# Block-sparse attention into a gated MLP: scores of batches 1 to 3 as pairs of 64-row products, their mask as two more

## The chip, the cores and the metric

The kernel runs on one core of one Trainium2 chip. The metric is the device time of one launch in microseconds (us), given as the median of several runs. The core's engines are named as the profile names them: PE is TensorE's matmul stream, PEld its weight loads, DVE VectorE, ACT ScalarE, POOL GpSimd, SP SyncE, which here issues transfers.

## The reference: what is computed

Attention over `q`, `k`, `v` of shape (4 batches, 8 heads, 768 positions, 64), then an MLP with a gate over the positions:

```python
scores = scale * q @ k^T                     # scale = 1/8
scores = where(mask, scores, -1e9)           # mask by blocks of 32 positions
attn   = softmax(scores)
x      = (attn @ v), heads side by side      # (4, 768, 512)
h      = max(x @ w_in, 0);  u, v = halves of h
v_n    = (v - mean(v)) / sqrt(var(v) + 1e-6)
v_s    = w_spatial @ v_n + b_spatial         # over the positions
out    = (u * v_s) @ w_out
```

A query block may look at its own and the neighbouring blocks, at the first and the last block, and at three sampled blocks; the first and last query blocks look at all. The sampled blocks are an input, the same for all batches and heads.

## The kernel before, in words

**The mask inside the score product.** A score needs 64 rows of the array (the head's width). `kq` is the scores' operand, a tile [128 partitions, 8 heads, 768 keys + 768 queries]: rows 0 to 63 hold a head's keys and queries, transposed, and rows 64 to 127 hold mask rows, for the keys a one at their block's row (24 blocks) and for the queries 0 or -300 for that block. One product over all 128 rows so gives score plus mask, and the exponential on ACT (which multiplies by 1/8) turns masked scores into nothing. The mask rows are built once, during batch 0, for each of the eight heads' places (`mask_rows`, line 268, and `rows`, line 236). In `mask_rows` line 269 is called three times; one of its calls uses only the 24 rows from 64 on.

**Slots.** The work is laid out by hand in slots, one loop at the end (line 846). Slots 0 to 35 (S0 = 36) are batch 0, in units cut for an early start. From slot 36 on each slot is one call of `qk_full(j, ci)` (line 422): for head j and one of six chunks of 128 keys, two products give 128 x 768 scores in a PSUM tile `ps` (two buffers), and one exponential writes them to `a_all`. There are 144 such slots, for 24 heads of batches 1 to 3. Seven slots later `av_full(j, qc)` (line 471) takes six products with `a_all` as weights and `vv` as the moving operand, one for each key chunk, to get 128 queries' output (65 columns: 64 and the row sum), and `normalize` (line 438) divides on DVE. Behind that, in the same slot, `run_queue` (line 712) issues MLP products of the batch before, dealt evenly over the slots: on average somewhat over two of up to 512 columns. So a slot's order on PE is: two score products, six value products, some MLP products, and PE takes them in that order.

**How keys and queries get to `kq` from batch 1 on.** The heads go in pairs p (two heads each, 12 slots a pair; `slot_of(p)`, line 808, is the pair's first slot g). SP loads k, q and v, mostly 36 slots ahead; POOL casts them, mostly 24 slots ahead, to bf16 (`nat`, both heads of a pair side by side in 128 columns); `tr_dma(p)` (line 372) has SP issue a transposing transfer, 17 to 19 slots ahead for most pairs (15 for pair 4), into `tt` [128 partitions, 12 chunks, 128], two buffers. In `tt` rows 0 to 63 are the first head of the pair and rows 64 to 127 the second. `split(p, h)` (line 376) copies one head's half on DVE, through `dve_copy` (line 211), into rows 0 to 63 of that head's place in `kq`, three to five slots ahead.

**Queues.** SP's queue holds, in order, the loads, the transposing transfers, the transposes of the attention output (`xtr_dma`, line 507) and the stores.

**Start and end.** At the start PE runs filler products (line 179) until there is work. After the last score slot come the rest of batch 3's MLP products, some 30 us.

Of the kernel before, what the change touches and what calls it, by code (L numbers as in the profile page):

```python
# [10 lines left out]
FP32 = mybir.dt.float32  # L11
BF16 = mybir.dt.bfloat16
I32 = mybir.dt.int32
AF = mybir.ActivationFunctionType
ALU = mybir.AluOpType
# [11 lines left out]
def kernel(  # L27
# [16 lines left out]
    nc = tc.nc  # L44

    B, H, S, D = q.shape
# [3 lines left out]
    NCH = S // 128  # L50
# [6 lines left out]
    NG = H // 2  # L57
# [13 lines left out]
    work = ctx.enter_context(tc.tile_pool(name="work", bufs=1))  # L71
    psum = ctx.enter_context(tc.tile_pool(name="psum", bufs=1, space=bass.MemoryType.PSUM))
# [10 lines left out]
    kq = const.tile([128, H, 2 * S], BF16, name="kq")  # L83
# [3 lines left out]
    MX = slice(D, 128)  # L87
# [95 lines left out]
    def ts(out, in0, s1, o0, s2=None, o1=None):  # L183
        kw = {} if o1 is None else {"op1": o1}
        nc.vector.tensor_scalar(out=out, in0=in0, scalar1=s1, scalar2=s2, op0=o0, **kw)  # L185

    def tt_op(out, in0, in1, op):
        nc.vector.tensor_tensor(out=out, in0=in0, in1=in1, op=op)
# [21 lines left out]
    def dve_copy(o, i):  # L210
        nc.vector.tensor_copy(out=o, in_=i)  # L211
# [158 lines left out]
    tt = {}  # L370

    def tr_dma(p):
        tt[p] = work.tile([128, 2 * NCH, 128], BF16, tag="tt", bufs=2, name="tt")
        nc.sync.dma_start_transpose(out=tt[p], in_=nat.pop(p).rearrange("p c h d -> p (c h d)"))

    def split(p, h):
        src = tt[p].rearrange("x c n -> x (c n)")
        dve_copy(kq[0:D, (2 * p + h) % H, :], src[h * D:(h + 1) * D, :])


    a_ref, av_ref, x_ref, xn_ref, xt_ref = {}, {}, {}, {}, {}

# [4 lines left out]
    def qk_unit(u, e):  # L387
# [31 lines left out]
            ps = ps.rearrange("p (c n) -> p c n", c=len(parts))  # L419
        nc.scalar.activation(out=out, in_=ps, func=AF.Exp, scale=0.125)  # L420

    def qk_full(j, ci):
        if ci == 0:
            a_ref["h", j] = work.tile([128, NCH * S], BF16, tag="a_all", bufs=3,
                                      name="a_all").rearrange("p (c n) -> p c n", c=NCH)
        ps = psum.tile([128, 1024], FP32, tag="sc", bufs=2)
        for n0, n1 in ((0, 512), (512, S)):
            nc.tensor.matmul(out=ps[:, n0:n1],  # L428
                             lhsT=kq[:, j % H, ci * 128:(ci + 1) * 128],
                             rhs=kq[:, j % H, S + n0:S + n1], start=True, stop=True)  # L430
        nc.scalar.activation(out=a_ref["h", j][:, ci, :], in_=ps[:, 0:S], func=AF.Exp, scale=0.125)  # L431

    def av_tile(key, n):
        ps = psum.tile([128, 512], FP32, tag="av", bufs=2, name="ps_av")
        av_ref[key] = ps[:, 0:n * VA].rearrange("p (c d) -> p c d", d=VA)
        x_ref[key] = ps[:, 512 - TW // 2:512].bitcast(BF16)

    def normalize(ps, out, n):
        rc = work.tile([128, NCH, 1], FP32, tag="rc", bufs=2)
        nc.vector.reciprocal(out=rc[:, 0:n], in_=ps[:, :, D:VA])  # L440
        nc.vector.tensor_tensor(out=out, in0=ps[:, :, 0:D],  # L441
                                in1=rc[:, 0:n].to_broadcast([128, n, D]), op=ALU.mult)

    def av_unit(u, e):
        t, p = UNITS[u]
        if e == 0:
            av_tile(u, 2 * TC)
        for i in range(8 * e, 8 * e + 8):
            g, ci = divmod(i, NCH)
            if t == "h":  # L450
                h, qc, to, n = p, g, g, 2 * TC
                pp = 0
            else:
                (h, qc), n, pp = divmod(g, TC), TC, p
                to = qc * 2 + h
            at = (h * NCH + ci) * n * 128 if t != "h" else ci * n * 128
            at += qc * 128
            nc.tensor.matmul(out=av_ref[u][:, to, :], lhsT=a_ref[u][:, at:at + 128],  # L458
                             rhs=vv[pp % NVV][:, h, ci, :],
                             start=(ci == 0), stop=(ci == NCH - 1))  # L460
        if e == 2:
            a_ref.pop(u)
            if t == "h":
                if p == 0:
                    xn_ref[0] = work.tile([128, 2 * TC, 2, D], BF16, tag="xn0", bufs=1, name="xn0")
                normalize(av_ref.pop(u), xn_ref[0][:, :, p, :], 2 * TC)
            else:
                xn_ref[u] = work.tile([128, TC, 2, D], BF16, tag="xn3", bufs=3, name="xn3")
                normalize(av_ref.pop(u), xn_ref[u].rearrange("p c h d -> p (c h) d"), 2 * TC)

    def av_full(j, qc):
        p, h = divmod(j, 2)
        if qc == 0:
            av_tile(j, NCH)
        for ci in range(NCH):
            nc.tensor.matmul(out=av_ref[j][:, qc, :],  # L476
                             lhsT=a_ref["h", j][:, ci, qc * 128:(qc + 1) * 128],
                             rhs=vv[p % NVV][:, h, ci, :],
                             start=(ci == 0), stop=(ci == NCH - 1))
        if qc == NCH - 1:  # L480
            a_ref.pop(("h", j))
            if h == 0:
                xn_ref["p", p] = work.tile([128, NCH, 2, D], BF16, tag="xn", bufs=2, name="xn")
            normalize(av_ref.pop(j), xn_ref["p", p][:, :, h, :], NCH)

    def xt_tile(p):
        if p not in xt_ref:
# [224 lines left out]
    def run_queue():  # L712
        if not queue or pace["slots"] <= 0:
            return
        pace["credit"] += (len(queue) - pace["credit"]) / pace["slots"]
        pace["slots"] -= 1
        n = int(pace["credit"] + 0.5)
        for _ in range(min(n, len(queue))):
            queue.popleft()()
            pace["credit"] -= 1  # L720
# [3 lines left out]
    at, late, pre = {}, {}, {}  # L724

    def when(slot, *fns):
        at.setdefault(slot, []).extend(fns)

    def c(f, *a, **kw):
        return lambda: f(*a, **kw)  # L730
# [77 lines left out]
    def slot_of(p):  # L808
        return S0 + 12 * (p - NG)

    for p in range(NG, NP):
        g = slot_of(p)
        when({4: 14, 5: 20, 6: 28, 11: g - 29, 15: g - 29}.get(p, g - 36), c(load, p, "k"), c(load, p, "q"), c(load, p, "v"))
        when({4: 17, 5: 23, 6: 37, 11: g - 22, 15: g - 22}.get(p, g - 24),
             *[c(cast, p, nm, PL, cs=cs) for nm in "kqv" for cs in (((C01, C23, C45) if p > 5 else (ALLC,)))])
        when({4: 21, 5: 27, 11: g - 18, 15: g - 18, 10: g - 17, 14: g - 17}.get(p, g - 19), c(tr_dma, p))
        if p % NG == 1 and p > 2 * NG:
            late.setdefault(g - 4, []).append(c(split, p, 0))
        else:
            when(g - 5, c(split, p, 0))  # L820
        when(g + 4 if p == NG else g - 3, c(split, p, 1))
        if p == NP - 1:
            when(g + 20, last_x)
        elif p % NG == NG - 1:
            when(g + 19, c(xtr_dma, p))
        else:
            when(g + 20, c(xtr_dma, p))
# [13 lines left out]
    for u in range(len(UNITS)):  # L841
        for e in range(3):
            sl = (5, 6, 6)[e] if u == 0 else 3 * u + e + (4 if u < 3 else 3)
            av_at.setdefault(sl, []).append((u, e))
    NS = S0 + 12 * (NP - NG)
    for s in range(NS + LAG + 2):
        if s < S0:
            qk_unit(*divmod(s, 3))
        elif s < NS:
            j, ci = divmod(s - S0, NCH)  # L850
            qk_full(j + H, ci)
        early = at.get(s, [])
        for f in pre.get(s, []):
            f()
        for u, e in av_at.get(s, []):
            av_unit(u, e)
        if 0 <= s - LAG - S0 and s - LAG < NS:
            j, qc = divmod(s - LAG - S0, NCH)
            av_full(j + H, qc)
        for f in early:  # L860
            f()
        run_queue()
        for f in late.get(s, []):
            f()
        while post:
            post.pop(0)()
# [31 lines left out]
```

## Time and profile before

| what | value |
|---|---|
| median of 3 runs | 210.06 us (209.74 to 210.12) |
| span of the profiled execution, first to last instruction | 208.3 us |
| its own time as a whole | not given; the runs lie 1.4 to 1.8 us above the span |
| instructions | 5489 |
| ACT exponentials of the 144 slots (line 431) | 144 x 812 ns, 113.4 us |
| PE products of the scores (line 428) | 288, 70.3 us with overlaps counted once |
| PE value products (line 476) | 864 of 65 columns |

How to read it: the profile counts an engine's busy time from its instructions' records. Records of PE products overlap, since a product starts before the one before it has ended, and their ends are modelled; the step from one start to the next says what a product costs in a stream. The chain of waits follows the work that ended last back to the start. The granted clock (PEclk) is the share of full speed at which PE was let run. In instruction rows `128*128` is rows x columns of the weights, then the moving operand.

### The profile page before, as it was taken

To read this page: it belongs to the slowest core of one execution; us is meant where nothing else is said; L and a number is where in the kernel's file an instruction comes from. 1 tells how busy PE (TensorE), PEld (TensorE's weight loads), DVE (VectorE), ACT (ScalarE), POOL (GpSimd) and SP (SyncE) were. 2 spreads that over 40 slices of the span, in tenths; PEclk is the share of its full clock that TensorE was granted. 3 is DMA by queue.
4 is the path that set the end of the run, shared out by engine and by line. 5 is a ranking of instruction groups with operands and counts; after the bars stand their busy time and mean duration, and the time that the engine had idled before them with its cause. 6 is when DMAs were issued, how large, how long until landed. Compare 5 with 4: busy or idle time off the path is not lost.

```text
span 208.3 us, 5489 instructions
## 1 busy us (share of the span) xinstructions
PE 201.0 (97%) x2203; PEld 138.0 (66%) x2225; DVE 146.8 (70%) x315; ACT 168.4 (81%) x222; POOL 89.4 (43%) x186
## 2 busy tenths in 40 slices
PE   6899999999999999999999999999999999999993
PEld 6599888777766776667556676667665567445551
DVE  6888776989876766575975585456875666576871
ACT  6899999999999999989899878889899884266021
POOL 6888989767927964006757600006210000013000
PEclk9999999999999999999999999999999999999999
DMA  5999899999999999499987920499402010610016
GB/s 143 338 362 357 275 383 270 206 247 389 253 253 308 259 300 208 139 199 386 292 176 206 139 41 0 164 189 335 75 0 41 0 37 4 250 57 0 0 70 232
DMA packets 53053, 39.48 MB, mean 190 GB/s; under 512 B 33956, under 2 KB 47652, under 8 KB 53028
## 3 DMA queue, kind: packets, MB, share of 16 engines
q1 hardware_dynamic: 52596, 38.74, 70.0%
q10 hardware_dynamic: 432, 0.39, 0.6%
q8 instruction: 17, 0.28, 0.5%
q14 instruction: 8, 0.07, 0.1%
HBM read 24.77 MB, written 6.29 MB: 149 GB/s over the span
## 4 chain that ended last, share of the span: by engine, by line
PE 87%; DVE 4%; ACT 4%; DMA 2%; issue 1%; POOL 0%; ACTq 0%
PE ps L428 21%; PE ps_moe L630 17%; PE ps_moe L561 13%; PE ps_av L476 12%; PE ps L415 7%; PE ps_av L458 4%; PE ps_t L561 4%; PE ps_t L630 4%; PE ps_sc L630 2%; ACT a_all L420 2%; DVE stats L594 2%; DVE vn L185 2%; DMA st_q<-in_q_dram 2%; PE ps_sc L561 1%; PE ps L263 1%
## 5 line engine op out<-in xcount | busy, mean ns | idle before, releaser
L431 ACT ACTIVATE a_all<-ps 128x768 bf16<-128x768 f32 x144 | 113.4, 812 | 13.8 <-PE ps L428 6.2
L428 PE MATMUL ps<-kq 128*128 128x512 bf16 (+1 forms) x288 | 70.3, 326 | 0.3
L476 PEld LDWEIGHTS <-a_all 128*128 128x128 bf16 x864 | 46.6, 98 | 19.0
L476 PE MATMUL ps_av<-vv,a_all 128*128 128x65 bf16 x864 | 51.1, 194 | 0.1
L428 PEld LDWEIGHTS <-kq 128*128 128x128 bf16 x288 | 27.9, 97 | 23.6
L137 POOL CAST nat<-st_k 128x256 bf16<-128x256 f32 (+3 forms) x37 | 17.7, 509 | 38.7 <-DMA st_k<-in_k_dram 38.7
L420 ACT ACTIVATE a_all<-ps 128x1024 bf16<-128x1024 f32 x35 | 33.5, 1027 | 0.3
L630 PE MATMUL ps_moe<-w_spt,vn 128*128 128x512 bf16 (+1 forms) x144 | 33.1, 325 | 0.0
L598 POOL TENSOR_SCALAR std<-mv 128x3 f32<-128x3 f32 (+1 forms) x9 | 3.4, 376 | 48.7 <-DVE mv L595 48.5
L661 DVE TENSOR_TENSOR sb<-ps_moe,b_row 128x512 f32<-128x512 f32 x18 | 12.4, 690 | 14.5 <-PE ps_moe L630 14.2
L630 PE MATMUL ps_moe<-xt,w_in_t 128*128 128x256 bf16 (+1 forms) x108 | 21.7, 299 | 0.2
L415 PE MATMUL ps<-kq 128*128 128x256 bf16 x135 | 20.8, 275 | 0.8 <-DVE kq L211 0.6
L561 PE MATMUL ps_moe<-w_in_t,xt 128*128 128x512 bf16 x65 | 20.2, 378 | 0.2
L137 POOL CAST vv<-st_v 128x256 bf16<-128x256 f32 (+2 forms) x37 | 18.5, 533 | 3.9 <-DMA st_v<-in_v_dram 3.8
L137 POOL CAST nat<-st_q 128x256 bf16<-128x256 f32 (+2 forms) x41 | 19.2, 496 | 1.6 <-DMA st_q<-in_q_dram 1.5
L561 PE MATMUL ps_moe<-w_out_t,un 128*128 128x512 bf16 x64 | 19.4, 378 | 0.2
L441 DVE TENSOR_TENSOR xn<-ps_av,rc 128x384 bf16<-128x384 f32 (+1 forms) x36 | 18.5, 513 | 1.4 <-DVE rc L440 0.2
L664 DVE TENSOR_TENSOR un<-sb,un 128x512 bf16<-128x512 f32 x24 | 17.4, 727 | 1.5
L630 PEld LDWEIGHTS <-vn 128*128 128x128 bf16 x192 | 15.5, 97 | 4.4
L594 DVE BATCH_NORM_STATS2 stats<-vn 128x6 f32<-128x512 bf16 x24 | 16.5, 688 | 1.5 <-ACT vn L589 0.9
L211 DVE COPY osb<-ps_moe 128x512 f32<-128x512 f32 x12 | 8.3, 689 | 11.2 <-PE ps_moe L561 9.3
L211 DVE COPY kq<-tt 64x1536 bf16<-64x1536 bf16 x24 | 15.4, 641 | 0.6 <-DMA tt<-nat 0.2
(94 smaller groups left out, 241.6 us busy)
## 6 DMA issues: line engine op xcount, KB each, us to landing
out_dram<-osb SPq DMA_DIRECT2D x23, 256.0 KB, 2.1
st_k<-in_k_dram SPq DMA_DIRECT2D x15, 384.0 KB, 4.6
st_v<-in_v_dram SPq DMA_DIRECT2D x15, 384.0 KB, 6.2
st_q<-in_q_dram SPq DMA_DIRECT2D x12, 384.0 KB, 4.9
ws_f<-in_moe_w_spatial_dram SPq DMA_DIRECT2D x6, 384.0 KB, 5.5
w_f<-in_moe_w_in_dram SPq DMA_DIRECT2D x8, 256.0 KB, 6.3
w_f<-in_moe_w_out_dram SPq DMA_DIRECT2D x4, 256.0 KB, 5.4
st_q<-in_q_dram SPq DMA_DIRECT2D x3, 256.0 KB, 6.9
```

Of the source, the lines that this page charges most:

```text
L137: eng.tensor_copy(out=dst, in_=src)
L211: nc.vector.tensor_copy(out=o, in_=i)
L415: nc.tensor.matmul(out=ps[:, at:at + n * TW], lhsT=kq[:, h, ci * 128:(ci + 1) * 128], rhs=kq[:, h, qcols(t0, n)], start=True, stop=True)
L420: nc.scalar.activation(out=out, in_=ps, func=AF.Exp, scale=0.125)
L428: nc.tensor.matmul(out=ps[:, n0:n1], lhsT=kq[:, j % H, ci * 128:(ci + 1) * 128], rhs=kq[:, j % H, S + n0:S + n1], start=True, stop=True)
L431: nc.scalar.activation(out=a_ref["h", j][:, ci, :], in_=ps[:, 0:S], func=AF.Exp, scale=0.125)
L441: nc.vector.tensor_tensor(out=out, in0=ps[:, :, 0:D], in1=rc[:, 0:n].to_broadcast([128, n, D]), op=ALU.mult)
L476: nc.tensor.matmul(out=av_ref[j][:, qc, :], lhsT=a_ref["h", j][:, ci, qc * 128:(qc + 1) * 128], rhs=vv[p % NVV][:, h, ci, :], start=(ci == ...
L561: nc.tensor.matmul(out=ref["ps"][:, 0:w], lhsT=lhs(i), rhs=rhs(i), start=(i == 0), stop=(i == n - 1))
L594: nc.vector.bn_stats(out=stats, in_=self.vn[:, tcc, :])
L630: nc.tensor.matmul(out=o.rearrange("p (c t) -> p c t", c=n), lhsT=lhs(i)[:, (d0 + x) * 128:(d0 + x + 1) * 128], rhs=rhs(i), start=(i == 0) ...
L664: nc.vector.tensor_tensor(out=self.in_place(*area), in0=sb, in1=self.in_place(*area), op=ALU.mult)
```

## The change: what it does

From batch 1 on, a slot treats both heads of a pair and half of the queries (384), where it treated one head and all 768. It issues four products of 384 columns over 64 rows each: scores of the first head (rows 0 to 63), scores of the second (rows 64 to 127), then the mask onto the first and the mask onto the second, accumulated in the same places of PSUM. Keys and queries are read as the transposing transfer left them. `split` and its 24 calls go. The mask rows, till now in rows 64 to 127 of `kq` place 0, are copied once to rows 0 to 63 too (`mask_low`, slot 30). Pairs 4 and 5 still use the two `tt` buffers; later pairs are transposed straight into places 4 to 7 of `kq`, in turn. The outputs of the exponential, the value products and the normalised output are indexed to match; counts and sizes of these stay. `DVE_MASKED` is empty, so `mask_chunk`, `masks` and the branches on `by_dve` add nothing.

```diff
     def tr_dma(p):
-        tt[p] = work.tile([128, 2 * NCH, 128], BF16, tag="tt", bufs=2, name="tt")
+        if p < NG + 2:
+            tt[p] = work.tile([128, 2 * NCH, 128], BF16, tag="tt", bufs=2, name="tt")
+        else:
+            tt[p] = kq[:, 4 + (p - 2) % 4].rearrange("x (c n) -> x c n", n=128)
         nc.sync.dma_start_transpose(out=tt[p], in_=nat.pop(p).rearrange("p c h d -> p (c h d)"))
-
-    def split(p, h):
-        src = tt[p].rearrange("x c n -> x (c n)")
-        dve_copy(kq[0:D, (2 * p + h) % H, :], src[h * D:(h + 1) * D, :])
...
+    DVE_MASKED = ()
+    HW = S // 2
+
+    def mask_low():
+        dve_copy(kq[0:D, 0, :], kq[MX, 0, :])
...
     def qk_full(j, ci):
+        p, f = divmod(j, 2)
...
-        ps = psum.tile([128, 1024], FP32, tag="sc", bufs=2)
-        for n0, n1 in ((0, 512), (512, S)):
-            nc.tensor.matmul(out=ps[:, n0:n1],
-                             lhsT=kq[:, j % H, ci * 128:(ci + 1) * 128],
-                             rhs=kq[:, j % H, S + n0:S + n1], start=True, stop=True)
-        nc.scalar.activation(out=a_ref["h", j][:, ci, :], in_=ps[:, 0:S], func=AF.Exp, scale=0.125)
+        ps = psum.tile([128, 1024], FP32, tag="sc", bufs=2, name="ps_s").rearrange("p (h n) -> p h n", h=2)[:, :, 0:HW]
+        by_dve = ci in DVE_MASKED
+        for h in range(2):
+            r = slice(h * D, (h + 1) * D)
+            nc.tensor.matmul(out=ps[:, h], lhsT=tt[p][r, ci], rhs=tt[p][r, NCH + f * TW3:NCH + (f + 1) * TW3],
+                             start=True, stop=by_dve)
+        if not by_dve:
+            for h in range(2):
+                r = slice(h * D, (h + 1) * D)
+                nc.tensor.matmul(out=ps[:, h], lhsT=kq[r, 0, ci * 128:(ci + 1) * 128],
+                                 rhs=kq[r, 0, S + f * HW:S + (f + 1) * HW], start=False, stop=True)
+        a = a_ref["h", j][:, ci]
+        nc.scalar.activation(out=a, in_=ps, func=AF.Exp, scale=0.125)
...
     def av_full(j, qc):
-        p, h = divmod(j, 2)
+        p, f = divmod(j, 2)
+        ql, h = divmod(qc, 2)
...
-                             lhsT=a_ref["h", j][:, ci, qc * 128:(qc + 1) * 128],
+                             lhsT=a_ref["h", j][:, ci, h, ql * 128:(ql + 1) * 128],
...
-            normalize(av_ref.pop(j), xn_ref["p", p][:, :, h, :], NCH)
+            normalize(av_ref.pop(j), xn_ref["p", p][:, f * TW3:(f + 1) * TW3].rearrange("p c h d -> p (c h) d"), NCH)
...
-        if p % NG == 1 and p > 2 * NG:
-            late.setdefault(g - 4, []).append(c(split, p, 0))
-        else:
-            when(g - 5, c(split, p, 0))
-        when(g + 4 if p == NG else g - 3, c(split, p, 1))
...
+    when(30, mask_low)
```

More of the change, by code (lines that the diff above doesn't have):

```diff
@@ L420, in qk_unit, with mask_chunk @@
         nc.scalar.activation(out=out, in_=ps, func=AF.Exp, scale=0.125)
+    DVE_MASKED = ()
+    HW = S // 2
+    def mask_low():
+        dve_copy(kq[0:D, 0, :], kq[MX, 0, :])
+    def mask_chunk(ci):
+        ps = psum.tile([128, 1024], FP32, tag="sc", bufs=2, name="ps_m").rearrange("p (h n) -> p h n", h=2)[:, :, 0:HW]
+        for f in range(2):
+            r = slice(f * D, (f + 1) * D)
+            nc.tensor.matmul(out=ps[:, f], lhsT=kq[r, 0, ci * 128:(ci + 1) * 128],
+                             rhs=kq[r, 0, S + f * HW:S + (f + 1) * HW], start=True, stop=True)
+        ts(keep[:, ci].rearrange("p (f n) -> p f n", f=2), ps, -1.0, ALU.is_ge, TOP, ALU.mult)
@@ L422, in qk_full @@
     def qk_full(j, ci):
+        p, f = divmod(j, 2)
         if ci == 0:
             a_ref["h", j] = work.tile([128, NCH * S], BF16, tag="a_all", bufs=3,
-                                      name="a_all").rearrange("p (c n) -> p c n", c=NCH)
-        ps = psum.tile([128, 1024], FP32, tag="sc", bufs=2)
-        for n0, n1 in ((0, 512), (512, S)):
-            nc.tensor.matmul(out=ps[:, n0:n1],
-                             lhsT=kq[:, j % H, ci * 128:(ci + 1) * 128],
-                             rhs=kq[:, j % H, S + n0:S + n1], start=True, stop=True)
@@ L431, in qk_full @@
-        nc.scalar.activation(out=a_ref["h", j][:, ci, :], in_=ps[:, 0:S], func=AF.Exp, scale=0.125)
+                                      name="a_all").rearrange("p (c h n) -> p c h n", c=NCH, h=2)
+        ps = psum.tile([128, 1024], FP32, tag="sc", bufs=2, name="ps_s").rearrange("p (h n) -> p h n", h=2)[:, :, 0:HW]
[4 more added lines that the diff above has]
+                             start=True, stop=by_dve)
@@ new lines, in qk_full @@
+        if not by_dve:
[5 more added lines that the diff above has]
+        nc.scalar.activation(out=a, in_=ps, func=AF.Exp, scale=0.125)
+        if by_dve:
+            masks.append(lambda: tt_op(a, a, keep[:, ci:ci + 1, f * HW:(f + 1) * HW].to_broadcast([128, 2, HW]), ALU.min))
@@ L433, in av_tile @@
+        if ci == NCH - 1 and f == 1:
+            tt.pop(p)
+    masks = []
+    TW3 = NCH // 2
     def av_tile(key, n):
@@ L481, in av_full @@
             a_ref.pop(("h", j))
-            if h == 0:
+            if f == 0:
                 xn_ref["p", p] = work.tile([128, NCH, 2, D], BF16, tag="xn", bufs=2, name="xn")
-            normalize(av_ref.pop(j), xn_ref["p", p][:, :, h, :], NCH)
+            normalize(av_ref.pop(j), xn_ref["p", p][:, f * TW3:(f + 1) * TW3].rearrange("p c h d -> p (c h) d"), NCH)
     def xt_tile(p):
@@ L845 @@
     NS = S0 + 12 * (NP - NG)
+    when(30, mask_low)
+    for i, ci in enumerate(DVE_MASKED):
+        late.setdefault(30 + i, []).append(c(mask_chunk, ci))
     for s in range(NS + LAG + 2):
@@ L859 @@
             av_full(j + H, qc)
+        while masks:
+            masks.pop(0)()
         for f in early:
```

## The prediction

> **What bounds the kernel now.** First the page's first two parts: busy shares, and the span in 40 slices.
>
> ```profile
> PE 201.0 (97%) x2203; PEld 138.0 (66%) x2225; DVE 146.8 (70%) x315; ACT 168.4 (81%) x222; POOL 89.4 (43%) x186
> ...
> PE   6899999999999999999999999999999999999993
> PEclk9999999999999999999999999999999999999999
> ```
>
> TensorE (PE) is busy 97% of the span, in nearly every slice, at full granted clock. A busy PE need not be a full one, so I next ask where the changed products lie. The view of their source line gives shortest, median and longest in ns, then the first and last start in us:
>
> ```profile
> L428 PE MATMUL ps<-kq x288: 270/324/379, 40.3 to 172.8; 128*128 128x512 bf16 x144
> ```
>
> How much idle time PE has there, the windows view says (its sum over five windows from 40.3 to 172.8 us):
>
> ```profile
> core 0: us, PE busy (x) PEld busy (x) DVE busy (x) ACT busy (x) POOL busy (x), PEclk, DMA share, GB/s
> ...
> sum 132.50, PE 131.75 PEld 87.56 DVE 91.98 ACT 118.85 POOL 51.74; mean PE 26.35 PEld 17.51 DVE 18.40 ACT 23.77 POOL 10.35
> ```
>
> The 288 products of line 428 are those of batches 1 to 3: 144 slots, two products each, from 40.3 to 172.8 us, so 0.92 us a slot. In that stage PE idles 132.50 - 131.75 = 0.75 us in all. The other engines have room: DVE 40 us, ACT 14 us. To see whether "busy" means streaming, take the chain of work in order of time:
>
> ```profile
> 12.11 0.44 PE ps L415 x4
> 12.55 0.45 PE ps L263 x8
> ...
> 102.45 0.32 PE ps L428 x2
> 102.77 0.19 PE ps_av L476 x6
> 102.96 0.65 PE ps_moe L561 x3
> 103.61 0.33 PE ps L428 x2
> ```
>
> These give the price of one product within a stream: 0.44/4 = 0.110 us for 256 columns, 0.45/8 = 0.056 for 128, 0.65/3 = 0.217 for 512, and 0.32 to 0.33 for a score pair of 512 + 256. Price goes with columns; there are no gaps, and the weight loads cost nothing visible. So **in this stage any time added to or taken from PE's stream reaches the end one for one**, and what leaves another engine is worth at most the 0.75 us.
>
> **The change, part by part.** The sum is made on the profiled execution (span 208.3 us; the page gives no time of its own for the whole execution). The runs' median, 210.06, is 1.8 us above that span; I carry that over and add to 210.06.
>
> *Columns.* A slot had 512 + 256 columns over 128 rows. Now it has two score products of 384 columns, one on rows 0 to 63 and one on rows 64 to 127, and two mask products of the same sizes: 4 x 384 columns. By the stream prices, 384 columns are about 0.163 us (midway between 0.110 and 0.217). If the two halves of the rows stream at the same time, a slot costs 2 x 0.163 = 0.326 us, the same as the 0.32 to 0.33 before: **0**. If they go one after the other, it costs 4 x 0.163 = 0.652, or 0.326 more. The trace has a single product over fewer than half of the rows, and that ran alone, so no row says whether two run together. The bounds are 0 and 144 x 0.326 = 46.9 us. I take 0: the operands come from different partitions, the two outputs lie 512 columns apart, and the products are issued in turn (low, high, low, high) with no wait between them. The high end is a rival. The Trainium skill, "TensorE: Matmul & The Clock Gate", Part 3, says that products on different row groups run concurrently, starting some 4 ns apart; no run here shows it.
>
> *Switches.* Between two score groups stand the six value products (line 476) and the MLP products, all over 128 rows. So each slot now enters a 64-row form and leaves it: 288 switches. That lone product, the 24-row mask product of line 269, shows what entering costs. PE's timeline around it (start, length, operation; x2 merges two):
>
> ```profile
> 5.01 0.29 PE L276 MATMUL psq<-ident,nat 128*128 128x128 bf16 x2 [0.65 <-POOL nat L137]
> 5.14 0.28 PE L179 MATMUL wps<-warm 128*128 128x128 bf16 x2
> 5.34 0.28 PE L269 MATMUL mq<-kq,bm 24*128 24x256 bf16 x1
> ```
>
> The weight loads of the same stretch, the filler products by their source line, and ACT's timeline, for the operand:
>
> ```profile
> 5.08 0.15 PEld L179 LDWEIGHTS <-warm 128*128 128x128 bf16 x2
> 5.34 0.09 PEld L269 LDWEIGHTS <-bm 24*128 24x128 bf16 x1
> ```
>
> ```profile
> L179 PE MATMUL wps<-warm x32: 217/314/314, 1.0 to 5.2; 128*128 128x128 bf16 x32
> ```
>
> ```profile
> 3.46 0.84 ACT L214 ACTIVATE kq<-kq 64x768 bf16<-64x768 bf16 x1
> ```
>
> The two fillers end at 5.42, and the shortest take 0.22, so the second began at 5.20. In a stream its successor would begin 0.056 later, with its weights loaded ahead. Here neither the load nor the product began before 5.34, which is 0.14 later. The 24-row load waits for no semaphore, and the product's operand was ready at 3.46 + 0.84 = 4.30. So entering cost 0.14 - 0.056 = 0.084 us: the array seems to run empty first. The Trainium skill, "TensorEngine Tiling (Array Packing)", Key Properties, says that a change of tiling mode drains TensorE; it gives no figure and speaks of any change, so by it leaving would pay as well as entering. The row shows entering alone, at 0.084.
>
> Leaving is not shown: its bounds are 0 (like any product after another) and that 0.084. I take 0.084, the only row of a change of form, and because what has to run empty is the same array. On top of it, the weight load that can no longer run ahead shows. At least 0.01: the pair at 5.01, which starts after an idle stretch, takes 0.29 against the fillers' 0.28. At most a whole load, 0.097, as the view of line 428 has it:
>
> ```profile
> L428 PEld LDWEIGHTS <-kq x288: 95/97/98, 40.1 to 172.6; 128*128 128x128 bf16 x144
> ```
>
> I take 0.01, since it is a difference of starts and the 0.097 a duration that even streamed loads show. A switch is then 0.094 us, and 288 of them are **27.1 us**. Nothing hides that: PE has 0.75 us of idle time in the stage. ACT, DVE and the transfers get slack from it and cannot become later than PE.
>
> *Weights inside a group.* The mask's weights for rows 0 to 63 are loaded while the score product is still in those rows. Full-row loads do this all the time, so I take 0; with a whole load showing once a slot it would be 144 x 0.097 = 14.0 us. The Trainium skill, "TensorE: Matmul & The Clock Gate", Part 3, "What overlaps and what doesn't", says that a load overlaps running products only if its row group differs. For full rows this trace disagrees, since the streamed pairs above leave no room for a load; for 64 rows no run here shows it. By that rule the 14.0 us would come on top.
>
> *DVE.* The 24 copies from the transposed tile into the scores' operand go; one copy of that shape, the mask's, is added at slot 30. The page's row:
>
> ```profile
> L211 DVE COPY kq<-tt 64x1536 bf16<-64x1536 bf16 x24 | 15.4, 641 | 0.6 <-DMA tt<-nat 0.2
> ```
>
> DVE loses 15.4 us and gains 0.64, all beside a full PE. The most it can bring is the stage's 0.75 us, and less once PE is slower; I count 0. The normalised output now goes out as one run of 384 columns, not in two interleaved halves: at most some of DVE's time.
>
> *Transposes and SP.* Pairs 6 and later are transposed straight into four places of the operand tile. SP's transpose now also waits for the products that last read the place, and the scores wait for its landing instead of for a copy. The view of the old transpose's line:
>
> ```profile
> L374 SPq DMA_TRANSPOSE tt<-nat x12: 1423/2166/5675, 28.4 to 143.3; - x12
> DMA to landing us min/median/max: 4.0/5.2/9.3
> ```
>
> It is issued 17 to 19 slots ahead of use: 15.6 us at the least against 9.3 to land. By the code the place's last reader is 9 slots or more before the issue, so the loads and stores queued behind on SP do not stand still. I count 0. If that cover went, the loads would come later by the same amount, with 36 slots of lead of their own for most pairs.
>
> *ACT.* Same count and shape of exponentials, read as two runs of 384: 0. It has 14 us of room, and gains more.
>
> **Sum:** 210.06 + 0 + 27.1 + 0 = 237.2 us.
>
> **The rivals.**
>
> *Switches cost only on entering.* 144 x 0.084 = 12.1, so 222.2 us. For: the row shows entering only. Against: the full-row products need the same empty array.
>
> *Mask weights do not load ahead.* 237.2 + 14.0 = 251.2 us. For: a half of the rows may have no place for a second set of weights. Against: full-row loads show nothing.
>
> *The halves do not run together,* so that the change does not do what it says: 237.2 + 46.9 = 284.1 us. For: no row shows two products at once. Against: separate partitions and outputs.
>
> *No switch costs anything* (the other side). The 24-row load was then late for a reason of its own, and 64-row loads run ahead like others. PE's columns are equal, and the 24 copies off DVE give back up to the 0.75 us: 209.3 to 210.1, say 209.6 us. It decides from below 0.75/288 = 0.0026 us a switch. For: one row at the kernel's start is thin. Against: in that row nothing else was being waited for.
>
> **How the numbers follow.** Chances: forecast 0.55, entering only 0.13, mask weights 0.13, halves in turn 0.09, no cost 0.10. The likeliest is 237.2 us. The range reaches down to the entering-only case with no load showing, 222, and up to 288 switches with the drain and a whole load each, 288 x (0.084 + 0.097) = 52.1, so 262; it covers the mask-weight case and leaves out 0.09 + 0.10 = 0.19. A measurement of this kernel tells about 0.2% (0.4 us) from no change. The no-cost case is half faster by that, half the same: faster 0.05, same 0.05, slower 0.90.
>
> **What would show it.** In the changed kernel's timeline, a score group should begin about 0.09 us later after the last MLP product than that product's columns explain, and the first value product likewise after the mask products; low and high halves should start within hundredths of a microsecond of each other, and a group should take 0.33 us. Slots should be 0.92 + 0.19 = 1.11 us, the stage 160 us, ACT's idle time up by about as much as PE's loss, and DVE 15 us less busy. I am wrong if halves start 0.16 apart (in turn), if the mask products lag by more than 0.163 (weights), or if slots stay at 0.92 (no drain).

## The result, and the profile after

The changed kernel takes 240.49 us (median of 4 runs, 240.44 to 240.84) against 210.09 us (4 runs, 209.74 to 210.50): 1.145 times the time of before, 95% interval 1.143 to 1.147. The span of its profiled execution is 238.7 us, 30.4 us longer.

The busy shares on the page of the changed kernel, and its slices:

```profile
PE 231.0 (97%) x2487; PEld 116.9 (49%) x2513; DVE 134.2 (56%) x292; ACT 172.3 (72%) x222; POOL 84.1 (35%) x186
...
PE   8899999999999999999999999999999999999993
PEclk9999999999999999999999999999999999999999
```

PE is "97% busy" in both kernels, at full clock in both, and yet one of them wastes 30 us. A record of a product runs to its modelled end, well beyond its columns, so the pauses disappear under the records. What tells is the share of the weight loads, 66% before and 49% now. (The Trainium skill, "Trainium Kernel Development and Optimization", Best Practices, says to judge the distance to the limit by MFU, the share of the peak arithmetic that is reached, and by the weight loads' share, and not by the matmuls' busy time; as to the loads' share this pair of profiles agrees.) Not all of the fall is pauses: more loads now run side by side, so the loads' own time fell too, from 138.0 to 116.9 us.

Where the time went, by windows of the changed kernel (first all but the score stage, then the score stage):

```profile
core 0: us, PE busy (x) PEld busy (x) DVE busy (x) ACT busy (x) POOL busy (x), PEclk, DMA share, GB/s
...
sum 75.70, PE 69.75 PEld 50.76 DVE 54.44 ACT 49.49 POOL 37.06; mean PE 34.88 PEld 25.38 DVE 27.22 ACT 24.75 POOL 18.53
```

```profile
40.40:203.40 163.00, 161.28 (x1740) 66.11 (x1758) 79.76 (x159) 122.81 (x159) 47.02 (x113) 1.00 0.60 151
```

The same split of the kernel before:

```profile
sum 75.50, PE 68.99 PEld 50.19 DVE 54.52 ACT 49.38 POOL 37.67; mean PE 34.49 PEld 25.10 DVE 27.26 ACT 24.69 POOL 18.84
```

```profile
40.30:173.10 132.80, 132.05 (x1459) 87.84 (x1472) 92.28 (x181) 119.02 (x159) 51.74 (x113) 1.00 0.75 185
```

Start and end last as long as before (75.7 against 75.5 us). The stage with the 144 score slots went from 132.8 to 163.0 us: **30.2 us, 0.210 a slot**. DVE is 12.5 us less busy there, which nobody notices. (The prediction's 15 added up the copies' records; the busy time counts records that overlap once.)

Where in a slot it lies, the chain of the changed kernel says, in order of time:

```profile
119.16 0.27 PE ps_s L443 x2
119.43 0.16 PE ps_s L448 x2
119.59 0.29 PE ps_av L504 x6
119.89 0.43 PE ps_moe L589 x2
120.32 0.27 PE ps_s L443 x2
120.59 0.16 PE ps_s L448 x2
120.75 0.30 PE ps_av L504 x6
```

The MLP pair (line 589) costs 0.43, two products of 512 columns, as ever. The mask pair (line 448) costs 0.16: two products in the time of one, loads included. The score pair (line 443) costs 0.27, 0.11 more than the mask pair of the same size, and the six value products (line 504) 0.29 to 0.30 against 0.19 before. The extra thus stands in two places, where the form of the products changes: 0.11 + 0.10 = 0.21.

The timeline of PE in the changed kernel, and of its weight loads:

```profile
119.73 0.59 PE L589 MATMUL ps_moe<-w_in_t,xt 128*128 128x512 bf16 x2
120.25 0.34 PE L443 MATMUL ps_s<-kq 64*128 64x384 bf16 x2
120.43 0.33 PE L448 MATMUL ps_s<-kq 64*128 64x384 bf16 x2
120.68 0.37 PE L504 MATMUL ps_av<-vv,a_all 128*128 128x65 bf16 x6
```

```profile
120.25 0.10 PEld L443 LDWEIGHTS <-kq 64*128 64x128 bf16 x2 [0.42 <-issue]
120.26 0.10 PEld L448 LDWEIGHTS <-kq 64*128 64x128 bf16 x2
120.68 0.24 PEld L504 LDWEIGHTS <-a_all 128*128 128x128 bf16 x6 [0.32 <-issue]
```

One record of line 443 lasts 0.33, two merged ones 0.34: the halves start within 0.01 us of each other. *Entering:* the second MLP product began at 119.73 + 0.59 - 0.38 = 119.94 and streams 0.217, to 120.16; the first load and product of the next form come at 120.25, 0.09 later. *Leaving:* the mask pair began at 120.43 and streams 0.163, to 120.59; the first value load and product come at 120.68, 0.09 later. Before, loads ran ahead; here "issue" stands as the reason of the loads' idle time, so no semaphore that the profile shows held them. *Inside the group* the mask's weights are loaded at 120.26, while the score products stream.

### The profile page after: what moved, and what is told of

Its sections match the earlier page's. It is cut to its first block, busy times and chain, and to the rows that moved or that the text cites. A ratio compares the mean times of both kernels' runs of the same rounds, so it can differ in the third digit from the quotient of the medians.

```text
span 238.7 us, 6041 instructions
## 1 busy us (share of the span) xinstructions
PE 231.0 (97%) x2487; PEld 116.9 (49%) x2513; DVE 134.2 (56%) x292; ACT 172.3 (72%) x222; POOL 84.1 (35%) x186
## 4 chain that ended last, share of the span: by engine, by line
PE 96%; ACT 1%; issue 1%; DVE 0%; ACTq 0%; DVEq 0%
PE ps_av L504 18%; PE ps_s L443 16%; PE ps_moe L658 16%; PE ps_moe L589 12%; PE ps_s L448 10%; PE ps L413 6%; PE ps_av L485 4%; PE ps_t L589 3%; PE ps_t L658 3%; PE ps_sc L658 2%; PE wps L179 1%; PE ps_sc L589 1%; PE ps L263 1%; ACT a_all L418 1%; PE ps_av L263 1%
## 5 line engine op out<-in xcount | busy, mean ns | idle before, releaser
L451 ACT ACTIVATE a_all<-ps_s 128x768 bf16<-128x768 f32 x144 | 116.7, 811 | 40.1 <-PE ps_s L448 35.8
L504 PEld LDWEIGHTS <-a_all 128*128 128x128 bf16 x864 | 35.4, 98 | 44.7 <-issue 43.2
L504 PE MATMUL ps_av<-vv,a_all 128*128 128x65 bf16 x864 | 52.5, 196 | 0.1
L448 PE MATMUL ps_s<-kq 64*128 64x384 bf16 x288 | 46.9, 322 | 0.0
L443 PE MATMUL ps_s<-kq 64*128 64x384 bf16 x240 | 40.3, 333 | 1.0
L137 POOL CAST nat<-st_k 128x256 bf16<-128x256 f32 (+3 forms) x37 | 16.4, 471 | 57.8 <-DMA st_k<-in_k_dram 57.7
L443 PEld LDWEIGHTS <-kq 64*128 64x128 bf16 x240 | 11.5, 92 | 42.6 <-issue 42.6
L626 POOL TENSOR_SCALAR std<-mv 128x3 f32<-128x3 f32 (+1 forms) x9 | 2.1, 238 | 60.8 <-DVE mv L623 60.3
L185 DVE TENSOR_SCALAR vn<-ps_moe 128x512 bf16<-128x512 f32 x18 | 12.4, 690 | 12.7 <-PE ps_moe L589 10.6
L137 POOL CAST nat<-st_q 128x256 bf16<-128x256 f32 (+2 forms) x41 | 17.2, 447 | 5.5 <-DMA st_q<-in_q_dram 5.5
L467 DVE RECIPROCAL rc<-ps_av 128x6 f32<-128x6 f32 (+1 forms) x36 | 6.8, 188 | 20.2 <-PE ps_av L504 17.9
```

Source lines behind the costliest of these rows:

```text
L137: eng.tensor_copy(out=dst, in_=src)
L443: nc.tensor.matmul(out=ps[:, h], lhsT=tt[p][r, ci], rhs=tt[p][r, NCH + f * TW3:NCH + (f + 1) * TW3], start=True, stop=by_dve)
L448: nc.tensor.matmul(out=ps[:, h], lhsT=kq[r, 0, ci * 128:(ci + 1) * 128], rhs=kq[r, 0, S + f * HW:S + (f + 1) * HW], start=False, stop=True)
L451: nc.scalar.activation(out=a, in_=ps, func=AF.Exp, scale=0.125)
L504: nc.tensor.matmul(out=av_ref[j][:, qc, :], lhsT=a_ref["h", j][:, ci, h, ql * 128:(ql + 1) * 128], rhs=vv[p % NVV][:, h, ci, :], start=(ci ...
```

## The experiments

**All rows in place of halves.** The changed kernel with this edit (the lines of the mask pair, not printed here, go too):

```diff
         for h in range(2):
-            r = slice(h * D, (h + 1) * D)
-            nc.tensor.matmul(out=ps[:, h], lhsT=tt[p][r, ci], rhs=tt[p][r, NCH + f * TW3:NCH + (f + 1) * TW3],
-                             start=True, stop=by_dve)
...
+            nc.tensor.matmul(out=ps[:, h], lhsT=tt[p][:, ci], rhs=tt[p][:, NCH + f * TW3:NCH + (f + 1) * TW3],
+                             start=True, stop=True)
```

> Changed kernel with the four 64-row products of a slot replaced by two of 384 columns over all 128 rows (it leaves out the mask and adds the two heads' scores). Theory (each change between the 128-row and the 64-row form costs PE some 0.1 us, nothing else in the change costs anything): 768 columns a slot and no change of form, so the time of before, 209.3 to 210.5 us, lower end if the freed DVE copies are worth PE's idle time. Rival (the direct transposes, their waits or the new indexing of the outputs cost part of the 30 us): clearly above 212 us.

Measured: 210.18 us, 1.0009 times before (0.9996 to 1.0023). Direct transposes, their waits, the new indexing and the mask's copy cost nothing together, and DVE's relief brings nothing either. DVE's row on its page shows the relief, PE's that it buys nothing:

```profile
PE 201.6 (97%) x2203; PEld 138.4 (67%) x2225; DVE 134.9 (65%) x292; ACT 168.2 (81%) x222; POOL 85.2 (41%) x186
```

So all 30 us belong to the 64-row products.

**Doubling the changes of form, and the counterpart.** An extra product of 64 columns over 128 rows, in unused columns of the score tile (`spare`), between the pairs or, in the counterpart, behind the mask pair. In both runs each product starts anew (`start=True`), so the mask overwrites the scores; the four products keep their form and columns.

```diff
-                             start=True, stop=by_dve)
+                             start=True, stop=True)
+        nc.tensor.matmul(out=spare, lhsT=warm, rhs=warm[:, 0:64], start=True, stop=True)
         if not by_dve:
...
-                                 rhs=kq[r, 0, S + f * HW:S + (f + 1) * HW], start=False, stop=True)
+                                 rhs=kq[r, 0, S + f * HW:S + (f + 1) * HW], start=True, stop=True)
```

> Changed kernel with one extra product of 64 columns over all 128 rows put between a slot's score pair and its mask pair; each product starts anew, so the scores are overwritten by the mask. Theory: one more leaving and one more entering per slot, 0.10 + 0.10 us, and 0.03 us for the columns: 144 x 0.22 to 0.23, so 272 to 274 us. Rival (the cost is one fixed price per slot, for instance a late start of the group, not a price per change of form): only the columns, 244 to 246 us.

> As the run with the extra product between the pairs, but the product stands behind the mask pair, ahead of the value products, so that no change of form is added. Theory and rival alike: 144 x 0.03 us for its columns, 244 to 246 us. If it costs far more, the extra product itself and not its place is what costs.

Measured: 275.5 us between, 244.92 behind. The same product costs 0.03 us a slot in one place and 0.24 in the other; the difference is 30.6 us, 0.212 a slot. The chain of the run with the product between the pairs (score pair, extra, mask pair, value products):

```profile
131.12 0.27 PE ps_s L444 x2
131.39 0.14 PE ps_s L446
131.53 0.27 PE ps_s L450 x2
131.80 0.30 PE ps_av L506 x6
```

The mask pair now costs 0.27 instead of 0.16, since it has become an entry, and the small product 0.14, since it has become a leaving.

**One change of form put into the kernel before.** A product of 64 columns behind the score products of the kernel before, over 64 rows or over 128:

```diff
+        nc.tensor.matmul(out=ps[:, S:S + 64], lhsT=warm[0:D], rhs=warm[0:D, 0:64], start=True, stop=True)
         nc.scalar.activation(out=a_ref["h", j][:, ci, :], in_=ps[:, 0:S], func=AF.Exp, scale=0.125)
```

> The kernel before with one extra product of 64 columns over 64 rows (zeros, into unused columns of the score tile) behind each slot's score products in batches 1 to 3. Theory: one entering and one leaving per slot, 0.20 us, and 0.03 us for the columns: 210.1 + 144 x 0.22 to 0.23 = 242 to 243 us. Rival (the price belongs to pairs of halves or to what follows in them, not to the form): only the columns, 214 to 215 us.

> The kernel before with the same extra product of 64 columns behind each slot's score products, but over all 128 rows: the counterpart to the extra product over 64 rows. Both theories: 144 x 0.03 us for the columns, 214 to 215 us.

Measured: 244.04 us over 64 rows, 214.45 over 128. Half the rows, the same columns, and 29.6 us more, 0.205 a slot. This is nearly the whole price of the change (0.210), without pairs, masks on top of scores or transposes. The chains of the two runs, the extra product (line 431) and the value products behind it, over 64 rows and then over 128:

```profile
131.16 0.13 PE ps L431
131.29 0.30 PE ps_av L477 x6
```

```profile
131.76 0.03 PE ps L431
131.79 0.19 PE ps_av L477 x6
```

The run over 64 rows and the one with the product between the pairs came out 1 to 1.5 us above what I had expected, since I had set a change of form at 0.10 us and it costs somewhat more.

**Order of the four products.** Low score, low mask, high score, high mask:

```diff
-                             start=True, stop=by_dve)
-        if not by_dve:
-            for h in range(2):
-                r = slice(h * D, (h + 1) * D)
-                nc.tensor.matmul(out=ps[:, h], lhsT=kq[r, 0, ci * 128:(ci + 1) * 128],
-                                 rhs=kq[r, 0, S + f * HW:S + (f + 1) * HW], start=False, stop=True)
+                             start=True, stop=False)
+            nc.tensor.matmul(out=ps[:, h], lhsT=kq[r, 0, ci * 128:(ci + 1) * 128],
+                             rhs=kq[r, 0, S + f * HW:S + (f + 1) * HW], start=False, stop=True)
```

> Changed kernel with the order of a slot's four products low score, low mask, high score, high mask in place of low score, high score, low mask, high mask. Theory (PE starts products strictly in order; two run together only when neighbours in the queue are on different halves): low mask waits for low score, high score runs beside low mask, high mask waits for high score: three times 0.163 us in place of two, 240.5 + 144 x 0.16 = 263 to 265 us. Rival (each half takes its products from the queue on its own): unchanged, 240 to 241 us. If no two halves ran together at all, the order would not matter either, at 240 to 241 us.

Measured: 241.31 us. **My theory of the queue fell**: I expected 263 to 265. The timeline of this run (line 443 score, 445 mask):

```profile
131.55 0.34 PE L443 MATMUL ps_s<-kq 64*128 64x384 bf16 x2
131.72 0.33 PE L445 MATMUL ps_s<-kq 64*128 64x384 bf16 x2
```

Rows are merged in order of start: both scores come first, within 0.01 us, although the low mask stands ahead of the high score in the queue (the compiled program holds the four in the order of the source). The high half took its product past one that waited for the low half. (The Trainium skill, "TensorE: Matmul & The Clock Gate", Part 3, "What overlaps and what doesn't", has products start strictly in order; this run shows otherwise for products on different halves of the rows.) Had the halves not run together, the order would not have mattered either, but the starts exclude that.

**Without the mask pair.** The loop with `start=False` left out.

> Changed kernel without the two mask products (the mask is left out). Theory: the mask pair's step of 0.173 us a slot goes, the two changes of form stay: 240.5 - 144 x 0.173 = 215 to 216 us, so still slower than before with half of before's columns streamed. Rival (a good part of the 30 us comes from adding the mask product onto the score product, or from loading its weights late): the time falls well below, 209 us or less.

Measured: 217.25 us, 1.033 times before (1.031 to 1.035). The mask pair is worth 23.2 us, 0.161 a slot, and not 0.173: the 0.01 of the load that shows belongs to whichever pair enters first. With half the columns streamed, the kernel is still slower than before, since the changes of form stay.

**Two slots' scores together.**

```diff
-            j, ci = divmod(s - S0, NCH)
-            qk_full(j + H, ci)
+            if (s - S0) % 2 == 0:
+                for x in (s, s + 1):
+                    j, ci = divmod(x - S0, NCH)
+                    qk_full(j + H, ci)
```

> Changed kernel with the scores of two slots issued together in every second slot, so that 72 groups of eight products stand in place of 144 of four; the computation is complete. Theory: half of the changes of form go, 72 x 0.21 = 15 us, so 225 to 226 us, if ACT keeps up with two score tiles filled together; up to 232 us if it does not. Rival (a fixed price per slot or per score product): 240 to 241 us.

Measured: 226.12 us, 1.075 times before (1.073 to 1.078): 14.4 us less than the changed kernel for 72 groups fewer, 0.200 each. Its chain:

```profile
130.00 0.27 PE ps_s L443 x2
130.27 0.16 PE ps_s L448 x2
130.43 0.16 PE ps_s L443 x2
130.59 0.16 PE ps_s L448 x2
130.76 0.29 PE ps_av L504 x6
```

The group's second score pair costs 0.16 like any pair; only the first pays for entering.

**Two slots together, without masks.** Both edits above; what grouping would be worth if the mask cost PE nothing.

> As the run with two slots' scores together, without the mask products (the mask is left out): what grouping would give if the mask cost PE nothing. Theory: 226.1 - 144 x 0.163 = 202.6 us, below before, since two slots then stream 2 x 384 columns' time in place of 2 x 768 and pay one leaving and one entering, 0.21 us. Rival (ACT is now the bound: both score tiles are filled together, so each group waits for both exponentials): 1.0 us a slot, 215 us or more.

Measured: 207.34 us, 0.987 times before (0.984 to 0.990). It is below before, but 4.7 us short of the theory. PE's timeline has groups of two lengths:

```profile
120.99 0.56 PE L443 MATMUL ps_s<-kq 64*128 64x384 bf16 x4
...
123.06 0.50 PE L443 MATMUL ps_s<-kq 64*128 64x384 bf16 x4
```

In the longer one the second pair came late; it needs the second score tile back from ACT, which is 88% busy in the windows from 60 to 170 us (97.08 of 110). ACT's timeline there:

```profile
119.64 1.51 ACT L446 ACTIVATE a_all<-ps_s 128x768 bf16<-128x768 f32 x2 [0.55 <-PE ps_s L443]
```

The exponential that held the tile ended at 119.64 + 1.51 = 121.15, and the pair began 0.05 later. By the starts in the trace the second pair is late in 29 of the 72 groups, each time 0.05 us after that exponential's end, and these delays come to 4.7 us in all. So ACT, the expectation's rival, accounts for the shortfall, though it costs far less than the 215 us set for it.

**The mask on another engine.** The last run's order, with a mask operation on the exponential's output, three slots after the scores. The mask itself (`keep`) is made once, by 12 products in slots 30 to 35. The main lines of the first run's edit; the second has two of six key chunks on POOL (`ON_POOL = (2, 5)`) and multiplies (`ALU.mult`):

```diff
+    DVE_MASKED = (0, 1, 2, 3, 4, 5)
...
+    keep = kq[:, 1:4].rearrange("p h x -> p (h x)").rearrange("p (c n) -> p c n", n=S)
...
+    MASK_AGE, ON_POOL = 3, ()
+
+    def mask_op(a, k, ci):
+        eng = nc.gpsimd if ci in ON_POOL else nc.vector
+        eng.tensor_tensor(out=a, in0=a, in1=k, op=ALU.min)
```

In both runs the first of a half pair's six value groups reads the last two key chunks ahead of their mask, so that part of the mask is left out; the work is all there.

> Two slots' scores together, and the mask put on the exponential's output by DVE (the smaller of it and 0 or 1e30, three slots later) in place of PE's mask products; the computation is complete. PE's part by theory as without masks, 202 to 204 us. It depends on DVE: 144 operations on 128 x 768 in bf16, not timed so far; at 0.45 us each they add 65 us to its 134 and just fit, at 0.85 us they add 122 us and make DVE the bound, 250 us or more. Rival (even where DVE fits, its queue comes late for the MLP's results and PE waits): 206 us or more with PE idle on DVE.

> As the run with the mask on DVE, but as a product with 0 or 1, two of six key chunks on POOL and four on DVE; the computation is complete. If DVE was the bound, it loses a third of the mask work: with 0.45 us an operation 203 to 206 us, with 0.85 us some 215 to 225 us, and POOL must do its 48 operations within its 140 idle us. If DVE fitted already, no difference, unless the two engines slow each other.

Measured: 247.58 us with DVE alone, 294.01 with POOL's help. By source line, the mask operations and who waited for them, DVE alone and then with POOL:

```profile
L465 DVE TENSOR_TENSOR a_all<-a_all,kq x144: 524/552/989, 50.5 to 211.2; 128x768 bf16<-128x768 bf16 x144
...
  PEld L513: 27.3, 49
  PE ps_av L513: 21.4, 46
```

```profile
L465 POOL TENSOR_TENSOR a_all<-a_all,kq x48: 1627/1637/2082, 54.5 to 253.4; 128x768 bf16<-128x768 bf16 x48
...
  PEld L513: 58.4, 41
  PE ps_av L513: 53.2, 39
```

0.55 us each are more than DVE has free. My expectation set 65 us against DVE's 134 over the whole span, but 54 of those 134 lie outside the score stage, where no mask work can go: in the stage it is 79.76 + 144 x 0.55 = 159 us, more than PE's stream needs. From 60 to 180 us DVE is busy 110.68 of 120, and PE's value products wait for its masks (the last two lines: us in total, times). POOL's help, expected to bring 203 to 225 us, costs 46 us instead. One operation takes 1.64 us there, three times as long as on DVE, and PE's value products wait for the few on POOL longer than for the many on DVE. From 60 to 180 us of that run (busy time and mean of one in ns, then PE's idle time ahead of them and who ended it):

```profile
L513 PE MATMUL ps_av<-vv,a_all 128*128 128x65 bf16 x478 | 36.7, 210 | 32.3 <-POOL a_all L465 20.4 <-DVE a_all L465 11.7
```

In that stretch no engine is more than 73% busy (DVE 87.63 of 120 us). What else these masks hold up was not tried. So no version here beats the kernel before with the whole mask computed; the best of those with half-row scores takes 226 us.

## Why the prediction was right, step by step

*PE's stream is the bound, one for one:* right. The stage grew by 30.2 us and the rest by 0.2. The 0.75 us of idle PE that the prediction gave as a reason could not have shown it, though: by the same view PE idles 163.00 - 161.28 = 1.72 us in the changed kernel's stage, which holds 30 us of pauses. What bears it out are the steps from start to start and the all-rows run.

*Columns, two halves at the price of one:* right, and now shown. The choice made without a row (0, against 46.9 us) is settled by the starts within 0.01 us and by pairs of 0.16 us. The rival "halves in turn" is out.

*Entering and leaving, 288 x 0.094 = 27.1 us:* right in kind, 10% small in size. Entering had a row, leaving did not and was a bet; both turned out alike, 0.09 us before the next load. Measured by taking half of the groups away it is 0.200 a slot, by adding it to the kernel before 0.205, by doubling it 0.212, and the change itself has 0.210. The forecast of 0.188 read 0.084 off one event at a resolution of 0.01 us. The trace holds starts in ns: the second filler began at 5.192 and the 24-row product at 5.343, so the same working gives 0.151 - 0.056 = 0.095. The changed kernel has that pause again: from a slot's last 512-column MLP product to its score pair it is 0.311 us, against 0.216 in a stream. With 0.01 for the load that is 0.105 a change of form and 0.210 a slot. So the mis-sized term is the 0.084, by the rounding of its row; 0.02 us in 144 slots is the 3.3 us between 237.2 and 240.49. "Entering only" (222.2) and "no switch costs anything" (209.6) are out.

*A showing weight load, 0.01 and not 0.097:* right: of the score pair's 0.27 the mask pair's 0.16 and the pause of 0.09 leave 0.01 to 0.02.

*Mask weights load ahead, 0:* right. They load at 120.26 while score products stream, and the mask step is 0.16. The rule of the Trainium skill ("TensorE: Matmul & The Clock Gate", Part 3, "What overlaps and what doesn't"), that a load overlaps running products only on another row group, does not hold for these 64-row products any more than for full rows.

*DVE, transposes, SP, ACT at nothing:* right; the all-rows run shows their sum, 1.0009 times before (0.9996 to 1.0023).

The Trainium skill ("TensorEngine Tiling (Array Packing)", Key Properties) says that a change of tiling mode drains TensorE; the pauses in both directions, about 0.1 us each with the load that shows, agree. What the array does in these 0.09 us no run shows; "runs empty" remains the reading that fits.

## What to carry to other kernels

Two products on different halves of the rows do run in the time of one, but every change between full-row and half-row products stops the stream for about 0.1 us, here as long as 240 columns. So count the changes of form ahead of the columns: by these figures half-row products can pay only in long unbroken runs, or where they remove more columns than that. No run here shows them paying with the whole mask computed. Where PE is the bound, taking work off an engine with room brings nothing, and a busy share of 97% says nothing about pauses of 0.1 us: read the steps from start to start.

## What was not expected of the hardware

A product on one half of the rows started ahead of an earlier one in the queue that waited for the other half (241.31 us against the 263 to 265 expected). And in the run with POOL's masks, where PE's value products stood idle for 32.3 of 120 us, the granted clock fell. A window of that run:

```profile
60.00:180.00 120.00, 85.80 (x795) 40.28 (x800) 87.63 (x138) 63.05 (x86) 85.97 (x103) 0.81 0.45 118
```

0.81 of full speed is the mean from 60 to 180 us; windows of 10 us in it read from 0.67 to 1.00. The same stretch has 0.97 with the masks on DVE alone, and 1.00 in the kernel before and in the changed one. Where the clock is down the products are slower: after a wait of 4.75 us, two MLP products of 512 columns start about 0.4 us apart, against 0.217 in a stream. So a part of the 294 us is the clock. That the waiting lowers it fits, but no run here separates the two, or says how large the part is.
